# The last product of an attention and two-layer feed-forward kernel, done by Strassen's seven products on 2x2 blocks

## The chip, the cores and the metric

The kernel runs on one core of a Trainium2 chip. A core has TensorE for matrix products (PE in the profile; its weight loads are shown apart as PEld), VectorE (DVE), ScalarE (ACT), GpSimd (POOL), and SyncE (SP), which issues DMAs. Each engine runs its own queue of instructions in order, and engines wait for each other by semaphores. The metric is the time of one execution on the device, in microseconds (us); the median of three runs before the change is 658.35 us (657.65 to 659.39).

## The reference

All arrays are float32. Attention has 2 batches of 8 heads, 1152 positions and 64 dimensions per head; neighbouring queries are averaged in pairs, so 576 rows per batch come out. They are joined to x with 1152 rows and 512 columns, which goes through two feed-forward layers:

```
x  = softmax(mean_of_pairs(q) @ k.T / 8) @ v        # joined to 1152 x 512
xn = x / sqrt(mean(x*x) + 1e-6) * rms_g
y  = (silu(xn @ w_gate) * (xn @ w_val)) @ w_out      # 512 -> 1536 -> 512
h  = y @ w_in                                        # second layer: 512 -> 2048
g  = h * tanh(softplus(h))                           # mish
out = g @ w_out2                                     # 2048 -> 512
```

The change concerns the second layer: the last product, and how its two operands are prepared.

## The kernel before

To keep float32 accuracy on float16 operands, each operand is kept as two float16 halves: hi, the rounded value, and lo, what the rounding left. ScalarE writes hi (a copy), and `lo_op` (L136) writes lo as the difference of the value and hi, on GpSimd or VectorE. A product is then three matmuls: hi by hi, hi by lo, lo by hi (`mm3`, L573, and L711 to L713).

The program is written by hand in the order in which each engine gets its instructions (`tc.manual_schedule`, L785); nothing reorders it. Weights come through a line of jobs (`jobs`, `job_step`): each call of `job_step` does the last step of one job (`w_c`: hi on ScalarE, lo on GpSimd), the middle step of the next (`w_b`: two integer instructions on VectorE that put a word together from its two halves) and the first of the one after it (`w_a`: one ScalarE instruction), and starts a load ahead.

The stages, on the span's clock: attention up to about 250 us; the first layer's two products (`unit1`, 24 matmuls of 288 columns a unit) up to 395 us; the first layer's output product (`unit1o`, 16 units of 36 matmuls of 288 columns) up to 466.4 us, with the rest of the jobs for w_out and w_in beside it; and the last stage.

In the last stage the 1152 rows are taken in three chunks of 384 (`CH`). For each chunk and each of 16 blocks of 128 hidden columns (`F2`), `h_mm` (L663) does 12 matmuls of 384 columns into a PSUM bank; `h_act` (L677) applies mish on ScalarE; `h_4` (L683) writes hi on ScalarE (L686) and lo on VectorE (L687, by `lo_op`) into `g`. `o_part` (L700) multiplies 128 rows of g by two of the 16 blocks of w_out2, 512 columns a matmul, and adds up in a PSUM bank; after the last block ScalarE copies the bank out (L716) and SyncE issues the DMA to `out`. [...]

Of the kernel before, what the change touches and what calls it, by code (L numbers as in the profile page):

```python
# [35 lines left out]

# [5 lines left out]
def kernel(  # L42
# [39 lines left out]
    def pool(name, bufs, side="left", **kw):  # L82
        return tc.alloc_tile_pool(name=name, bufs=bufs, side=side, reuse_waits="tile", **kw)
# [331 lines left out]
    def w_a(job):  # L415
        t = job["raw"]
        gx = raw_p.tile([128, t.shape[1], t.shape[2]], F32, tag="gx", name="gx")
        hw = t[:, :, :, 1].bitcast(F32)
        if job.get("mish"):
            nc.scalar.activation(out=gx, in_=hw, func=ACTF.Copy, scale=2.0 ** -111)  # L420
        else:


            nc.scalar.activation(out=gx, in_=hw, func=ACTF.Prelu, scale=2.0 ** -111, alpha=-(2.0 ** 32))  # L424
        job["g"] = gx

    def w_b(job, part=None):

        t, g = job["raw"], job["g"].bitcast(I32)
        if part in (None, 0):  # L430
            job["c"] = raw_p.tile([128, t.shape[1], t.shape[2]], I32, tag="c", name="c")
        c = job["c"]
        if part in (None, 0):
            nc.vector.tensor_scalar(out=c, in0=t[:, :, :, 0], scalar1=29, scalar2=None,  # L434
                                    op0=ALU.logical_shift_right)
        if part in (None, 1):
            if job.get("mish"):
                nc.vector.scalar_tensor_tensor(out=c, in0=g, scalar=-0x80000000, in1=c,
                                               op0=ALU.bitwise_and, op1=ALU.bitwise_or)
                nc.vector.tensor_scalar(out=g, in0=g, scalar1=3, scalar2=0x7FFFFFFF,  # L440
                                        op0=ALU.logical_shift_left, op1=ALU.bitwise_and)
                nc.vector.tensor_tensor(out=c, in0=g, in1=c, op=ALU.bitwise_or)
            else:
                nc.vector.scalar_tensor_tensor(out=c, in0=g, scalar=3, in1=c,  # L444
                                               op0=ALU.logical_shift_left, op1=ALU.bitwise_or)
# [213 lines left out]
    def w2o_job(z):  # L659
        return {"load": lambda: w_load(words(w_out2)[z * 128:(z + 1) * 128, :].rearrange(  # L660
            "(k p) (f t) -> p k f t", p=128, t=2), 1),
            "to": lambda: (w2o[:, z:z + 1, 0, :], w2o[:, z:z + 1, 1, :]), "mish": True}

    gt, zt = {}, {}

    def h_mm(c, f):
        if f == 0:
            gt[c] = g_p.tile([128, F2, 2, CH], F16, tag="g", name="g")
        ps = ps_z.tile([128, 512], F32, tag="z", name="z")
        w, y1T = w2i[0], y1[0]  # L670
# [12 lines left out]
    def h_4(c, f):  # L683
        o = zt.pop((c, f))
        g = gt[c]
        nc.scalar.activation(out=g[:, f, 0, :], in_=o, func=ACTF.Copy, scale=G_S)  # L686
        lo_op(nc.vector, g[:, f, 1, :], o, G_S, g[:, f, 0, :])  # L687
# [10 lines left out]
    po_t = {}  # L698

    def o_part(c, t, part, parts):  # L700
        T = c * (CH // 128) + t
        if part == 0:
            po_t[T] = ps_o.tile([128, 512], F32, tag="o", name="po")
        ps = po_t[T]
        g = gt[c]
        n = F2 // parts
        for f in range(part * n, (part + 1) * n):
            w = w2o
            gh = g[:, f, 0, t * 128:(t + 1) * 128]
            gl = g[:, f, 1, t * 128:(t + 1) * 128]  # L710
# [3 lines left out]
        if part == parts - 1:  # L714
            o = ot_p.tile([128, DM], F32, tag="ot", name="ot")
            nc.scalar.activation(out=o, in_=ps, func=ACTF.Copy, scale=1.0 / (G_S * W_S))  # L716
            for p0, p1, dst in out_rows(T):
                nc.sync.dma_start(out=dst, in_=o[p0:p1, :])


    FL = [(0, 8), (8, 8), (16, 8), (24, 8), (32, 4)]
# [63 lines left out]
    with tc.manual_schedule():  # L785
# [113 lines left out]
        rest = [w2i_job(z) for z in range(F1 - 2 * NWB, NZ)]
        per = []  # L900
        for z in range(6, 3 * KD):
            per.append([wo_job(z)] + rest[0:1])
            rest = rest[1:]
        per += [[x] for x in rest]
# [19 lines left out]
        hs = [(c, f) for c in range(NC) for f in range(F2)]
        PARTS = 8
        NO = CH // 128
        os_ = [(c, t, p) for c in range(NC) for p in range(PARTS) for t in range(NO)]
        on = 0
        for hn in range(len(hs) + 2):
            if hn < len(hs):  # L930
                h_mm(*hs[hn])
            if 1 <= hn <= len(hs):
                h_act(*hs[hn - 1])
            if 2 <= hn:
                h_4(*hs[hn - 2])
            if jn[3] < len(jobs):
                job_step()
            goal = (hn - OLAG) * NO * PARTS // F2
            while on < min(goal, len(os_)):
                o_part(*os_[on], PARTS)  # L940
                on += 1
        while on < len(os_):
            o_part(*os_[on], PARTS)
            on += 1
        for p in (ot_p, m_p, g_p, ps_o, ps_z, w2i_p, y1_p, raw_p, const):
# [31 lines left out]
```

## Time and profile before

| | |
|---|---|
| median of three runs | 658.35 us |
| the profiled execution | 659.05 us |
| its span, first to last instruction | 657.3 us |
| PE busy | 597.6 us (91%), 5880 matmuls |
| DVE busy | 413.2 us (63%) |
| ACT busy | 391.7 us (60%) |
| POOL busy | 309.9 us (47%) |
| mean granted TensorE clock | 0.992 of full speed |

A row of the timeline gives start, duration, engine, source line, operation, written tile and read tiles, the shape, and how often it stands in a row; in square brackets stands how long the engine was idle before it and which instruction ended the wait. Matmuls overlap in the pipeline, so the time that a matmul takes from its stream is the distance of two starts, and not its duration. The execution's own time is 1.8 us longer than its span. Line numbers of the rows are those of the kernel before.

### The profile page before, as it was taken

The numbers are of one execution on the slowest core, as the hardware profiler recorded it, in microseconds if no ns is written. First come the engines' busy times: TensorE is split into PE (matmuls) and PEld (weight loads), VectorE is DVE, ScalarE is ACT, GpSimd is POOL, SyncE is SP. The second block draws the span as 40 slices with busy tenths as digits, with TensorE's granted clock in tenths as the row PEclk, the third lists the DMA queues.
The fourth block names the chain that finished last, engine by engine and source line by source line (L and its number), as shares of the span: only waits on it lengthen the run. The fifth ranks groups of instructions, "written<-read, shape, count | busy, mean of one in ns | idle before, by whom it ended". The sixth has DMA issues, their size and how long they took to land.

```text
span 657.3 us, 14631 instructions
## 1 busy us (share of the span) xinstructions
PE 597.6 (91%) x5880; PEld 419.1 (64%) x5880; DVE 413.2 (63%) x679; ACT 391.7 (60%) x661; POOL 309.9 (47%) x255
## 2 busy tenths in 40 slices
PE   3588989887887789899999999999999999999997
PEld 2366767666656567677777777777655555555553
DVE  4798989889998896568888311554499931111110
ACT  4799999998987886666666331442455533223221
POOL 0778988878896861567778420441233310000000
PEclk9899999999998999999999999999999999999999
DMA  6599999998999996545556202453244100001001
GB/s 195 133 184 202 203 192 186 210 194 183 174 209 217 181 177 143 145 145 176 172 183 192 65 1 65 130 184 105 85 140 153 41 17 32 1 2 48 1 1 48
DMA packets 161908, 84.05 MB, mean 128 GB/s; under 512 B 124720, under 2 KB 152368, under 8 KB 161840
## 3 DMA queue, kind: packets, MB, share of 16 engines
q1 hardware_dynamic: 151184, 67.71, 46.8%
q10 hardware_dynamic: 10656, 15.40, 7.8%
q8 instruction: 46, 0.75, 0.5%
q14 instruction: 22, 0.18, 0.1%
HBM read 50.07 MB, written 2.36 MB: 80 GB/s over the span
## 4 chain that ended last, share of the span: by engine, by line
PE 65%; ACT 14%; DVE 8%; issue 8%; POOL 2%; ACTq 1%; DMA 1%; DVEq 0%; POOLq 0%
ACT e L283 6%; PE z L576 5%; PE z L578 5%; PE z L577 5%; PE po L713 5%; PE po L712 5%; PE po L711 5%; PE pg L576 3%; PE pv L578 3%; PE pg L577 3%; PE pv L576 3%; PE pv L577 3%; PE pg L578 3%; PE py L576 3%; PE py L578 3%
## 5 line engine op out<-in xcount | busy, mean ns | idle before, releaser
L138 POOL TENSOR_TENSOR hl<-e,hl 128x768 f16<-128x768 f32 x71 | 117.9, 1663 | 55.8 <-ACT hl L296 26.8
L274 DVE CUSTOM_DVE_ANT_1 junk<-s,shift 128x1152 bf16<-128x1152 f32 x72 | 97.2, 1351 | 8.1 <-PE s L255 7.5
L283 ACT ACTIVATE e<-s,m 128x1152 f32<-128x1152 f32 x72 | 87.6, 1217 | 13.6 <-DVE m L274 12.8
L255 PE MATMUL s<-kqT 128*128 128x384 f16 (+1 forms) x480 | 85.4, 333 | 10.2 <-DVE kqT L209 8.1
L140 DVE SCALAR_TENSOR_TENSOR g<-mo,g 128x384 f16<-128x384 f32 x48 | 26.8, 562 | 93.3 <-ACT g L686 93.3
L138 POOL TENSOR_TENSOR stretch<-c,stretch 128x512 f16<-128x512 f32 x40 | 47.8, 1194 | 60.6 <-ACT stretch L451 60.3
L347 PE MATMUL av<-vv,et 128*128 128x65 f16 (+1 forms) x720 | 74.1, 193 | 0.9 <-DVE x L395 0.9
L349 PE MATMUL av<-vv,et 128*128 128x64 f16 (+1 forms) x720 | 74.0, 193 | 0.0
L350 PE MATMUL av<-vv,et 128*128 128x65 f16 (+1 forms) x720 | 73.9, 195 | 0.0
L347 PEld LDWEIGHTS <-et 128*128 128x128 f16 (+1 forms) x720 | 67.2, 101 | 2.4 <-issue 2.3
L349 PEld LDWEIGHTS <-et 128*128 128x128 f16 (+1 forms) x720 | 67.0, 100 | 0.7
L350 PEld LDWEIGHTS <-et 128*128 128x128 f16 (+1 forms) x720 | 67.1, 100 | 0.0
L434 DVE TENSOR_SCALAR c<-raw 128x512 int32<-128x512 int32 x68 | 48.2, 708 | 26.6 <-POOL woh L138 24.5
L138 POOL TENSOR_TENSOR h<-fo,h 128x288 f16<-128x288 f32 x48 | 45.0, 937 | 42.0 <-ACT h L613 42.0
L296 ACT ACTIVATE hl<-e 128x768 f16<-128x768 f32 x72 | 60.6, 842 | 3.9 <-POOL khl L138 1.8
L576 PE MATMUL z<-y,w2i 128*128 128x384 f16 x192 | 62.6, 326 | 0.0
L577 PE MATMUL z<-y,w2i 128*128 128x384 f16 x192 | 62.6, 326 | 0.0
L578 PE MATMUL z<-y,w2i 128*128 128x384 f16 x192 | 62.6, 326 | 0.0
L680 ACT ACTIVATE mo<-z 128x384 f32<-128x384 f32 x48 | 23.2, 484 | 64.1 <-PE z L578 63.9
L444 DVE SCALAR_TENSOR_TENSOR c<-gx,c 128x512 int32<-128x512 int32 x52 | 57.7, 1110 | 4.1 <-ACT gx L424 2.2
L255 PEld LDWEIGHTS <-kqT 128*128 128x128 f16 (+1 forms) x480 | 39.7, 101 | 31.7 <-issue 13.5
L576 PE MATMUL pg<-stretch 128*128 128x288 f16 x192 | 54.9, 286 | 2.1 <-DMA stretch<-xh 1.6
(110 smaller groups left out, 1549.1 us busy)
## 6 DMA issues: line engine op xcount, KB each, us to landing
raw<-in_moe_w_out_dram SPq DMA_DIRECT2D x28, 512.0 KB, 3.4
raw<-in_moe_w_in_dram SPq DMA_DIRECT2D x16, 512.0 KB, 3.9
raw<-in_moe_w_gate_dram SPq DMA_DIRECT2D x8, 512.0 KB, 3.5
raw<-in_moe_w_val_dram SPq DMA_DIRECT2D x8, 512.0 KB, 3.8
vn<-in_v_dram ACTq DMA_DIRECT2D x14, 288.0 KB, 4.4
kn<-in_k_dram ACTq DMA_DIRECT2D x12, 288.0 KB, 4.1
qn<-in_q_dram ACTq DMA_DIRECT2D x12, 256.0 KB, 3.8
raw<-in_moe_w_gate_dram ACTq DMA_DIRECT2D x4, 512.0 KB, 4.7
```

The source lines that it names most:

```text
L138: eng.tensor_tensor(out=out_, in0=in_, in1=hi, op=ALU.subtract)
L255: mm = nc.tensor.matmul(out=ps[p0:p0 + m, c, 0:SN], lhsT=qt[:, w * NTI + slot, p0:p0 + m], rhs=kt[:, e * NJ + c * per:e * NJ + (c + 1) * p ...
L274: nc.vector.tensor_tensor_reduce(out=junk.rearrange("p (c s) -> p c s", c=SC), in0=ps[:, :, 0:SN], in1=shift.unsqueeze(2).to_broadcast([12 ...
L283: nc.scalar.activation(out=e.rearrange("p (c s) -> p c s", c=SC), in_=ps[:, :, 0:SN], func=ACTF.Exp, bias=m, scale=s_scale)
L296: nc.scalar.activation(out=t[:, 0, :], in_=e_t[n][:, 0:NB * 128], func=ACTF.Copy)
L347: nc.tensor.matmul(out=av[0:m, o0:o0 + D + 1], lhsT=hi, rhs=vr[:, D:2 * D + 1], start=(jj == 0), stop=False)
L349: nc.tensor.matmul(out=av[0:m, o0:o0 + D], lhsT=hi, rhs=vr[:, 0:D], start=False, stop=False)
L350: nc.tensor.matmul(out=av[0:m, o0:o0 + D + 1], lhsT=et[:, z + (NB if jj < NB else PB), p0:p0 + m], rhs=vr[:, D:2 * D + 1], start=False, st ...
L444: nc.vector.scalar_tensor_tensor(out=c, in0=g, scalar=3, in1=c, op0=ALU.logical_shift_left, op1=ALU.bitwise_or)
L576: nc.tensor.matmul(out=ps, lhsT=w0, rhs=x0, start=(i == 0), stop=False)
L577: nc.tensor.matmul(out=ps, lhsT=w0, rhs=x1, start=False, stop=False)
L578: nc.tensor.matmul(out=ps, lhsT=w1, rhs=x0, start=False, stop=(i == n - 1))
```

## The change

The last product, g (1152 x 2048) by w_out2 (2048 x 512), is taken in blocks. Two blocks of 128 rows (an index `q` from 0 to 3; the ninth block of rows, `q` = 4, stays as it is) by two halves of the hidden columns, and two halves of the hidden columns by two halves of the 512 output columns, are 2x2 blocks of blocks. Plain multiplication takes eight block products for each; Strassen's scheme takes seven products of sums of blocks, and sums of the results. A block product is now 24 matmuls of 256 columns (`product`, 8 steps `i` of the halved inner length by three matmuls).

What it adds for that:
- `h_mm(q, u)` does two blocks of hidden columns for 256 rows: 24 matmuls of 256 columns into one bank; for `q` = 4, 48 matmuls of 128 columns.
- `h_act` applies mish to 512 elements, and GpSimd then makes four sums or differences of the blocks in three instructions (128, 256 and 128 elements, float32); the next two wait for the one before.
- `h_4`, three turns behind `h_mm` (before: two), writes hi and lo of seven blocks, 896 elements, instead of 384. The tile that mish and the sums share has four buffers.
- Of w_out2 three blocks are used as they are (`w2b`) and four as sums (`w2t`). `w2_sums(i)` makes the sums on VectorE (512, 256 and 256 elements, two operands in SBUF); `w2_parts(i)` writes hi on ScalarE (1024 elements) and lo on GpSimd, for i = 1, 4 and 7 on VectorE. Eight of each; the first two sums ahead of the loop, the others and the parts in its first 15 turns.
- `o_end` combines a product into the results: the first product is copied out by ScalarE (tile `p1`), the others are added by VectorE. The pool of banks for these products has three.
- The order of the seven products is such that those without sums of weights (`y` under 3) come first.
- The 16 jobs of w_out2 move into the stage before, beside `unit1o`; the remaining ten jobs of w_in move ahead of that into the first layer. [...]

The order of the loop is now: 8 turns `h` of q = 0, 8 of q = 1, 7 products of q = 0, 8 turns of q = 2, 7 products of q = 1, and so on.

```diff
-    def o_part(c, t, part, parts):
...
-            nc.tensor.matmul(out=ps, lhsT=gh, rhs=w[:, f, 0, :], start=(f == 0), stop=False)
-            nc.tensor.matmul(out=ps, lhsT=gh, rhs=w[:, f, 1, :], start=False, stop=False)
-            nc.tensor.matmul(out=ps, lhsT=gl, rhs=w[:, f, 0, :], start=False, stop=(f == F2 - 1))
...
+    def w2_sums(i):
+        b = w2f[:, i].rearrange("p h (n d) -> p (h n) d", n=2)
+        t = w2s[i] = tt_p.tile([128, 4, NHF], F32, tag="tt", name="tt")
+        for z, x, y in ((slice(0, 2), b[:, 0:1].to_broadcast([128, 2, NHF]), b[:, 1:3]), (2, b[:, 2], t[:, 0]),
+                        (3, b[:, 3], t[:, 2])):
+            nc.vector.tensor_tensor(out=t[:, z], in0=x, in1=y, op=ALU.subtract)
+    def w2_parts(i):
+        t, o = w2s.pop(i), w2t[0][:, i]
+        nc.scalar.activation(out=o[:, 0], in_=t, func=ACTF.Copy)
+        lo_op(nc.vector if i % 3 == 1 else nc.gpsimd, o[:, 1], t, 1.0, o[:, 0])
...
+            nc.scalar.activation(out=t[:, 0:4, :], in_=ps.rearrange("p (s t) -> p s t", s=4), func=ACTF.Mish, scale=sc)
+            nc.gpsimd.tensor_tensor(out=t[:, 4], in0=t[:, 0], in1=t[:, 2], op=ALU.add)
+            nc.gpsimd.tensor_tensor(out=t[:, 5:7], in0=t[:, 0:8:4], in1=t[:, 1:2].to_broadcast([128, 2, 128]), op=ALU.subtract)
+            nc.gpsimd.tensor_tensor(out=t[:, 7], in0=t[:, 3], in1=t[:, 6], op=ALU.subtract)
...
+            t = t[:, 1:8, :]
+            hi, lo = g[:, u, 0], g[:, u, 1]
+        nc.scalar.activation(out=hi, in_=t, func=ACTF.Copy, scale=G_S)
+        lo_op(nc.vector, lo, t, G_S, hi)
...
+    def product(ps, g, x, y, start, stop):
+        w, y = (w2b[0], y) if y < 3 else (w2t[0], y - 3)
+        for i in range(FP):
+            gh, gl = g[:, i, 0, x, :], g[:, i, 1, x, :]
+            wh, wl = w[:, i, 0, y, :], w[:, i, 1, y, :]
+            nc.tensor.matmul(out=ps, lhsT=gh, rhs=wh, start=start and i == 0, stop=False)
+            nc.tensor.matmul(out=ps, lhsT=gh, rhs=wl, start=False, stop=False)
+            nc.tensor.matmul(out=ps, lhsT=gl, rhs=wh, start=False, stop=stop and i == FP - 1)
+    SEVEN = [(0, 0), (2, 2), (6, 1), (5, 5), (4, 4), (3, 3), (1, 6)]
...
+        if z == 0:
+            t = keep["p1"] = ot_p.tile([128, NHF], F32, tag="p1", name="p1")
+            nc.scalar.activation(out=t, in_=ps, func=ACTF.Copy, scale=sc)
...
+        ps_z = pool("ps_z", 5, space=PSUM)
+        ps_o = pool("ps_o", 3, space=PSUM)
+        f_p = pool("f4", 4)
+        tt_p = pool("tt", 2)
...
+        for n, (kind, q, z) in enumerate(line):
+            (h_mm if kind == "h" else o_mm)(q, z)
+            if last and last[0] == "h":
+                h_act(*last[1:])
+            if len(hq) > 1 or (hq and kind == "o"):
+                h_4(*hq.pop(0))
+            if last and last[0] == "h":
+                hq.append(last[1:])
+            if last and last[0] == "o":
+                o_end(*last[1:])
+            if wp and n % 2 == 0:
+                w2_parts(wp.pop(0))
+            elif ws:
+                w2_sums(ws.pop(0))
+            last = (kind, q, z)
```

On GpSimd, at the start of the last stage, there stood only the lo halves of the weights before (stretch is where w_out2 lies):

```order
L138 TENSOR_TENSOR woh<-c,woh 128x4x128
L138 TENSOR_TENSOR w2i<-c,w2i 128x4x128 x5
L138 TENSOR_TENSOR stretch<-c,stretch 128x512 x16
L972 UNCONDITIONAL_BRANCH
L972 ISA
```

Now there stand, in the same place, the lo halves of w2b, and then, for each unit, the three sums of its tile f, with the lo halves of w2t between them:

```order
L139 TENSOR_TENSOR w2b<-stretch,w2b 128x768 x5
L139 TENSOR_TENSOR w2t<-tt,w2t 128x1024
L726 TENSOR_TENSOR f_7636<-f_7636 128x128
L727 TENSOR_TENSOR f_7636<-f_7636 128x256
L728 TENSOR_TENSOR f_7636<-f_7636 128x128
L726 TENSOR_TENSOR f_7670<-f_7670 128x128
L727 TENSOR_TENSOR f_7670<-f_7670 128x256
L728 TENSOR_TENSOR f_7670<-f_7670 128x128
```

GpSimd, which had 16 instructions in the whole stage, has its instructions of each unit between the mish and the hi half of that unit.

On VectorE a turn of the first units was, before, one lo half of g and four instructions of a w_out2 job:

```order
L140 SCALAR_TENSOR_TENSOR g<-mo,g 128x384
L434 TENSOR_SCALAR c<-raw 128x512
L438 SCALAR_TENSOR_TENSOR c<-gx,c 128x512
L440 TENSOR_SCALAR gx<-gx 128x512
L442 TENSOR_TENSOR c<-gx,c 128x512
```

Now it is the lo half of g, larger, and in every second turn the sums of weights in tile tt; here are the turns that follow the lo half of part 1:

```order
L139 TENSOR_TENSOR w2t<-tt,w2t 128x1024
L141 SCALAR_TENSOR_TENSOR g<-f_7636,g 128x896
L679 TENSOR_TENSOR tt<-stretch 128x512
L679 TENSOR_TENSOR tt<-stretch,tt 128x256 x2
L141 SCALAR_TENSOR_TENSOR g<-f_7670,g 128x896
L141 SCALAR_TENSOR_TENSOR g<-f_7702,g 128x896
L679 TENSOR_TENSOR tt<-stretch 128x512
L679 TENSOR_TENSOR tt<-stretch,tt 128x256 x2
```

Every one of these instructions reads two operands from SBUF.

On ScalarE, around the first products, these rows stand now (f4 is the tile of mish and sums, stretch the g of q = 1, p1 the copy of the first product); the first two hi halves are those of the units 13 and 14, the third that of unit 15:

```order
L740 ACTIVATE stretch_89<-f4_8085 128x896
L740 ACTIVATE stretch_89<-f4_8119 128x896
L802 ACTIVATE p1_8186<-po_8126 128x256
L740 ACTIVATE stretch_89<-f4_8151 128x896
L725 ACTIVATE f4_8379<-z_8327 128x512
L725 ACTIVATE f4_8409<-z_8354 128x512
```

Before, a copy of a finished bank stood there every 16 units and more (L716); now the copy of the first product's bank stands behind the hi half of unit 14.

## Rows read from the trace of the kernel before

**Rows 1.** Busy time by stretch: stretch, length, PE, PEld, DVE, ACT, POOL, clock, DMA.
```profile
500.00:520.00 20.00, 20.00 (x109) 10.52 (x108) 19.41 (x28) 10.82 (x23) 6.55 (x6) 1.00 0.30 106
580.00:600.00 20.00, 20.00 (x109) 10.53 (x108) 2.58 (x5) 3.61 (x8) 0.00 (x0) 1.00 0.00 1
```
**Rows 2.** Groups of PE in the last stage: count, busy us, mean ns, idle.
```profile
L576 PE MATMUL z<-y,w2i 128*128 128x384 f16 x192 | 62.6, 326 | 0.0
...
L711 PE MATMUL po<-stretch,g 128*128 128x512 f16 x144 | 54.6, 379 | 0.0
```
**Rows 3.** Timeline of PE: start, duration, at several places of the span.
```profile
201.10 0.28 PE L204 MATMUL s<-ident,khl 128*128 128x128 f16 x2
...
201.55 0.28 PE L318 MATMUL ep<-idf,e 128*128 128x128 f32 x1
...
466.39 0.33 PE L576 MATMUL z<-y,w2i 128*128 128x384 f16 x1
...
644.81 0.38 PE L711 MATMUL po<-stretch,g 128*128 128x512 f16 x1
...
653.01 0.38 PE L713 MATMUL po<-stretch,g 128*128 128x512 f16 x1
```
**Rows 4.** Timeline of DVE and POOL where both work on SBUF.
```profile
414.94 1.16 POOL L138 TENSOR_TENSOR w2i<-c,w2i 128x512 f16<-128x512 f32 x1
417.92 1.71 POOL L138 TENSOR_TENSOR woh<-c,woh 128x512 f16<-128x512 f32 x1 [1.82 <-ACT woh L451]
...
415.02 1.36 DVE L434 TENSOR_SCALAR c<-raw 128x512 int32<-128x512 int32 x1 [16.02 <-POOL woh L138]
...
417.46 0.42 DVE L434 TENSOR_SCALAR c<-raw 128x512 int32<-128x512 int32 x1
417.91 0.69 DVE L444 SCALAR_TENSOR_TENSOR c<-gx,c 128x512 int32<-128x512 int32 x1
...
19.11 1.64 POOL L138 TENSOR_TENSOR hl<-e,hl 128x768 f16<-128x768 f32 x1 [17.17 <-ACT hl L296]
20.70 1.62 POOL L169 TENSOR_TENSOR qs<-qn 128x576 f32<-128x576 f32 x1
...
19.91 1.16 DVE L145 TENSOR_SCALAR kn<-kn 128x576 f32<-128x576 f32 x1
```
**Rows 5.** Durations: groups of ACT and DVE, and one line of POOL (ns, min/median/max).
```profile
L686 ACT ACTIVATE g<-mo 128x384 f16<-128x384 f32 x48 | 24.7, 516 | 0.0
...
L296 ACT ACTIVATE hl<-e 128x768 f16<-128x768 f32 x72 | 60.6, 842 | 3.9 <-POOL khl L138 1.8 <-ACT e L283 0.2
...
L140 DVE SCALAR_TENSOR_TENSOR g<-mo,g 128x384 f16<-128x384 f32 x48 | 26.8, 562 | 93.3 <-ACT g L686 93.3
...
L442 DVE TENSOR_TENSOR c<-gx,c 128x512 int32<-128x512 int32 x16 | 11.1, 693 | 0.6
...
L169 POOL TENSOR_TENSOR qs<-qn x7: 1397/1414/1845, 20.7 to 190.8; 128x576 f32<-128x576 f32 x7
```
**Rows 6.** Timeline at the start of the last stage.
```profile
466.59 0.41 ACT L644 ACTIVATE y<-py 128x288 f16<-128x288 f32 x1 [4.00 <-PE py L578]
...
467.02 1.28 ACT L923 ACT_TABLE_LOAD   x1
...
467.86 0.69 DVE L444 SCALAR_TENSOR_TENSOR c<-gx,c 128x512 int32<-128x512 int32 x1
```
**Rows 7.** Timeline of PE in the first layer's output product.
```profile
434.84 0.29 PE L578 MATMUL py<-h,woh 128*128 128x288 f16 x1
435.29 0.28 PE L576 MATMUL py<-h,woh 128*128 128x288 f16 x1 [0.16 <-DVE y L140]
```
**Rows 8.** Busy time by stretch, as in rows 1, where the clock changes.
```profile
26.60:33.20 6.60, 5.23 (x22) 2.81 (x21) 3.88 (x8) 4.89 (x8) 5.71 (x4) 0.50 0.67 151
202.70:206.10 3.40, 0.81 (x10) 0.39 (x7) 3.40 (x5) 0.92 (x2) 1.12 (x2) 1.00 1.17 244
207.50:210.70 3.20, 3.20 (x34) 2.16 (x31) 2.20 (x4) 3.17 (x5) 1.91 (x2) 0.50 0.92 237
```

More of the change, by code (lines that the diff above doesn't have):

```diff
@@ L32 @@
 NE, JOB0, JOBL = 4, 59, 55
-OLAG = 6
 PB = 3
@@ L418, in w_a @@
         hw = t[:, :, :, 1].bitcast(F32)
[L419 to L424, printed above, removed]
+        nc.scalar.activation(out=gx, in_=hw, func=ACTF.Prelu, scale=2.0 ** -111, alpha=-(2.0 ** 32))
         job["g"] = gx
@@ L436, in w_b @@
         if part in (None, 1):
[L437 to L445, printed above, removed]
+            nc.vector.scalar_tensor_tensor(out=c, in0=g, scalar=3, in1=c,
+                                           op0=ALU.logical_shift_left, op1=ALU.bitwise_or)
             del job["raw"], job["g"]
     def w_c(job):
+        if "to" not in job:
+            job["end"]()
+            return
         hi, lo = job["to"]()
@@ L669, in h_mm, with col0, g_buf @@
+    gt, zt = {}, {}
+    NQ = NT // 256
+    def col0(q):
+        return NI * 128 if q == NQ else q * 256 + (128 if q >= NI // 2 else 0)
+    def g_buf(q):
+        if q not in gt:
+            if q % 2:
+                gt[q] = stretch[:, 0:FP * 2 * 7 * 128].rearrange("p (i w s t) -> p i w s t", i=FP, w=2, s=7)
+            else:
+                gt[q] = g_p.tile([128, FP, 2, 7, 128], F16, tag="g", name="g")
+        return gt[q]
+    def h_mm(q, u):
         ps = ps_z.tile([128, 512], F32, tag="z", name="z")
@@ L683, in h_4 @@
[L683 to L687, printed above, removed]
+        n = 128 if q == NQ else 256
+        cs = slice(col0(q), col0(q) + n)
+        fs = [u + FP * h for h in range(2)] if n == 256 else [i + FP * h for i in (2 * u, 2 * u + 1) for h in range(2)]
+        for z, f in enumerate(fs):
+            mm3(ps[:, z * n:(z + 1) * n], lambda i: (w[:, i, 0, f * 128:(f + 1) * 128], w[:, i, 1, f * 128:(f + 1) * 128]),
+                lambda i: (y1T[:, i, 0, cs], y1T[:, i, 1, cs]), KD)
@@ L689, in out_rows, with h_4 @@
+    def h_4(q, u):
+        t = zt.pop((q, u))
+        g = g_buf(q)
+        if q == NQ:
+            t = t[:, 0:6, :].rearrange("p (i s) t -> p i s t", i=2)
+            hi, lo = [g[:, 2 * u:2 * u + 2, w, 0:3, :] for w in range(2)]
+        else:
+            t = t[:, 1:8, :]
+            hi, lo = g[:, u, 0], g[:, u, 1]
+        nc.scalar.activation(out=hi, in_=t, func=ACTF.Copy, scale=G_S)
+        lo_op(nc.vector, lo, t, G_S, hi)
     def out_rows(T):
@@ L696, in out_rows @@
         return [(0, TL, out[TB - TL:TB, :]), (TL, 128, out[2 * TB - TL:2 * TB, :])]
-    po_t = {}
-    def o_part(c, t, part, parts):
[L701 to L710, printed above, removed]
-            nc.tensor.matmul(out=ps, lhsT=gh, rhs=w[:, f, 0, :], start=(f == 0), stop=False)
-            nc.tensor.matmul(out=ps, lhsT=gh, rhs=w[:, f, 1, :], start=False, stop=False)
-            nc.tensor.matmul(out=ps, lhsT=gl, rhs=w[:, f, 0, :], start=False, stop=(f == F2 - 1))
-        if part == parts - 1:
-            o = ot_p.tile([128, DM], F32, tag="ot", name="ot")
-            nc.scalar.activation(out=o, in_=ps, func=ACTF.Copy, scale=1.0 / (G_S * W_S))
+    acc, keep = {}, {}
@@ new lines, with o_mm, o_end, plus @@
+    SEVEN = [(0, 0), (2, 2), (6, 1), (5, 5), (4, 4), (3, 3), (1, 6)]
+    ODD = [(0, 0), (1, 2), (2, 1), (0, 4)]
+    def o_mm(q, z):
+        x, y = (ODD if q == NQ else SEVEN)[z]
+        if q < NQ or z % 2 == 0:
+            acc[q] = ps_o.tile([128, 512], F32, tag="o", name="po")
+        product(acc[q][:, 0:NHF], gt[q], x, y, q < NQ or z % 2 == 0, q < NQ or z % 2 == 1)
+        acc[q, z] = acc[q][:, 0:NHF]
+    def o_end(q, z):
+        ps = acc.pop((q, z))
+        sc = 1.0 / (G_S * W_S)
+        def plus(to, x):
+            if isinstance(to, str):
+                t = keep[to] = ot_p.tile([128, NHF], F32, tag=to, name=to)
+            else:
+                t = to
+            nc.vector.scalar_tensor_tensor(out=t, in0=ps, scalar=sc, in1=keep[x], op0=ALU.mult, op1=ALU.add)
+        def send(T, o):
@@ L890 @@
             jobs += [wo_job(f - 2 * NWB), w2i_job(f - 2 * NWB), w1_job(f, 0), w1_job(f, 1)]
+        jobs += [w2i_job(z) for z in range(F1 - 2 * NWB, NZ)]
         units = [(f, c) for f in range(NWB) for c in range(NH // B + 1, NH)]
@@ L898 @@
         unit1_end(*done1[-1])
[L899 to L904, printed above, removed]
+        jw = [w2o_job(i, h) for i in range(FP) for h in range(2)]
+        jo = [wo_job(z) for z in range(6, 3 * KD)]
+        turns = "ww w o ow o ww o ow o ww ww w w w w w".split()
+        for x in "".join(turns):
+            jobs.append((jo if x == "o" else jw).pop(0))
         outs = [(d, c) for d in range(KD) for c in range(NH)]
@@ L907 @@
             unit1o(d, c)
-            if i < len(per):
-                jobs += per[i]
-                job_step(len(per[i]))
+            job_step(len(turns[i]))
             if i:
@@ L913 @@
         unit1o_end(*outs[-1])
-        jobs += [w2o_job(z) for z in range(F2)]
-        for p in (ps_f, ps_t, ps_av, wo_p, h1_p, h0_p, ftm):
+        job_step(2)
+        for p in (ps_f, ps_t, ps_av, wo_p, h1_p, h0_p, ftm, raw_p):
             p.release()
@@ L918 @@
         ps_o = pool("ps_o", 3, space=PSUM)
-        g_p = pool("g", 2)
-        m_p = pool("m", 3)
-        ot_p = pool("ot", 2)
-        nc.scalar.preload_act_table_set("mish")
[L924 to L945, printed above, removed]
+        w2t_p = pool("w2t", 1)
+        w2t[0] = w2t_p.tile([128, FP, 2, 4, NHF], F16, tag="w2t", name="w2t")
+        g_p = pool("g", 1)
+        f_p = pool("f4", 4)
+        tt_p = pool("tt", 2)
+        ot_p = pool("ot", 1)
+        nc.scalar.preload_act_table_set("mish")
+        line = []
+        for q in range(NQ + 1):
+            line += [("h", q, u) for u in range(FP if q < NQ else FP // 2)]
+            if q:
+                line += [("o", q - 1, z) for z in range(7)]
+        line += [("o", NQ, z) for z in range(4)]
+        hq, last = [], None
+        for i in range(2):
+            w2_sums(i)
+        wp, ws = list(range(FP)), list(range(2, FP))
+        for n, (kind, q, z) in enumerate(line):
[13 more added lines that the diff above has]
+            last = (kind, q, z)
+        o_end(*last[1:])
+        for p in (ot_p, tt_p, f_p, g_p, w2t_p, ps_o, ps_z, w2b_p, w2i_p, y1_p, const):
             p.release()
```

79 lines of the change are left out of this document (60 added, 19 removed).

## The prediction

> **What bounds the kernel now.** I read the table by stretch first: in the last stage PE is busy for 20.00 us of each 20, at full clock, both while the weights' jobs still keep DVE at 19.41 and after them, when DVE needs 2.58 and POOL nothing [rows 1]. So the stage lasts as long as PE's stream, and the other engines have room. Then the groups of PE: 3 x 192 matmuls of 384 columns and 3 x 144 of 512 [rows 2]. Then the distances of starts in the timeline: 38 matmuls of 512 columns from 644.81 to 653.01, 216 ns each; eight of 128 columns from 201.10 to 201.55, 56 ns each [rows 3]. Both are columns/2.4 plus about 2.5 ns, so 384 columns take 162.5 ns and 256 take 109.2. Check: 576 x 0.1625 + 432 x 0.2159 = 186.9 us; from 466.39, the stage's first matmul, that gives 653.3, where the last one of 653.01 ends its turn [rows 3]. Last I looked where DVE and POOL work side by side.
>
> **PE's own work.** After: h takes 768 matmuls of 256 and 192 of 128 columns, 768 x 0.1092 + 192 x 0.056 = 94.6 us; the products take 28 x 24 + 4 x 24 = 768 of 256, 83.9. Together 178.5, so PE saves 8.4 us if it never waits.
>
> What goes out of the stage, the w_out jobs with DVE's 19.41 of 20 us, was hidden under PE's full stream [rows 1] and brings nothing by itself.
>
> **The stage before.** PE lost 0.33 us at 434.84 to 435.29, where a bank was late: its reader came after a wait of ScalarE for a weight buffer [rows 7]. The jobs of w_out now stand in later turns, behind more of those readers; I count 0.3 saved. The other moved jobs run beside PE's full stream; nothing of them is waited for before their last, at the stage's start.
>
> **What DVE and POOL do to each other.** A POOL instruction of 512 elements takes 1.16 us; the one at 417.92, started 0.01 after a DVE one of 0.69 with two SBUF operands, took 1.71: it ended 1.02 after DVE's end. A DVE instruction of 0.42, started at 415.02 beside POOL's of 414.94, took 1.36 and ended 0.28 after POOL's. So one waits for the whole of the other, and hides only 0.14 us of its own in the wait. Where POOL has a queue, they take turns: DVE's of 19.91 ended 0.32 after POOL's first, and POOL's second took 1.62 where 1.40 is the least [rows 4, 5]. The change's new instructions on both engines are of this kind.
>
> Durations. POOL: 512 and 768 elements take 1.16 and 1.64 [rows 4], 1.9 ns an element and 0.18 us; with two float32 operands 576 take 1.40 [rows 5], 2.12 ns an element. So 128, 256 and 128 take 0.45 + 0.72 + 0.45 = 1.62 a unit, and a lo half of 1024 2.14. That no row shows float32 sums this small is a bound: at 1.9 ns a unit takes 1.51. DVE: 384 take 0.562 and 512 take 0.693 [rows 5], 1.04 ns an element and 0.16, so SBUF is held 0.93 for 896 and 1.07 for 1024. ScalarE: 384 in 0.516, 768 in 0.842 [rows 5], so 896 in 0.95, 1024 in 1.06. With some 0.6 for a mish of 512 ScalarE needs 0.95 + 0.6 and every second turn 1.06, some 2.1 of PE's 2.62 a turn: it is late only where it waits.
>
> **Where it is late.** Time 0 is the first matmul of the stage; a turn of PE is 24 x 0.1092 = 2.62 us. The first products need g of q = 0, ready with unit 7, half way through the sum below. The latest thing is a bank: the fourth product takes the bank of the first, which ScalarE reads into p1, in its queue behind the hi half of unit 14, and that waits for POOL's sums of unit 14. PE is there after 16 units and three products, at 19 x 2.62 = 49.8.
>
> POOL's start: y's hi half begins at 0.2, the last job's word is ready on DVE at 2.2 (467.86 + 0.69) [rows 6]; ScalarE's w2b half 0.84, POOL's lo of it 1.64, to 4.8. Beside it ScalarE loads its table, 1.28, to 4.4; DVE makes the first weight sums, held up by that POOL instruction, to about 5.2; w2t's hi half 1.06; POOL begins with w2t at 6.4. To the end of unit 14 it has five lo halves and 15 units: 5 x 2.14 + 15 x 1.62 = 35.0. In that time DVE takes SBUF for 14 lo halves of g, six sums of weights and three lo halves of w2t: 14 x 0.93 + 6 x 1.07 + 3 x 1.07 = 22.7, in 14 + 18 + 3 = 35 instructions, and each wait hides 0.14: 4.9. So POOL ends unit 14 at 6.4 + 35.0 + 22.7 - 4.9 = 59.2. With 0.08 to start, hi of 0.95, and p1's 256 elements in 0.37, the bank is free at 60.6: PE waits 10.8 us.
>
> Bounds of that. If POOL's start-up parts always fell into DVE's turns, and its sums went at 1.9 ns, POOL needs 45 x 0.04 + 15 x 0.97 + 5 x 2.0 + 22.7 = 49.1, and PE waits 7.1. If none is hidden, 57.7 + 6.4 = 64.1, and it waits 15.7. A gain from the wait is excluded, since p1 cannot pass in ScalarE's queue. I take 10.8, nearest to the rows, where waits did hide 0.14. After it POOL needs less than a turn (1.62 + 0.93 against 2.62, and the seven products give it 18 us more), so I expect no second wait of this size.
>
> **The clock.** PE was idle for most of 202.7 to 206.1, at a granted clock of 1.00; in 207.5 to 210.7, with PE full again, it was 0.50, the lower of the two levels, 1.2 GHz; an earlier stretch at that level, 26.6 to 33.2, is twice as long [rows 8]. After a wait of ten us I expect the same, 3.2 to 6.6 us of work at half rate, 1.6 to 3.3 us lost. I take 2.5.
>
> **The end.** The last copy is 0.2 shorter; a second DMA (the ninth block of rows goes to two places) is issued behind it. Bounds -0.4 and +0.4; I take 0.
>
> **Sum.** -8.4 - 0.3 + 10.8 + 2.5 = +4.6 us. Against the profiled execution, 659.05, that is 663.6 (its span 657.3 to 661.9). The median of the runs is 0.7 lower: 662.9.
>
> **Rivals.**
> A second forecast, faster: POOL and DVE take no turns, or POOL's float32 sums slip between. Place: the same bank. POOL's queue alone ends at 6.4 + 35.0 = 41.4, p1 at 42.8, ahead of PE's 49.8. It decides from the point where POOL ends unit 14 before 48.4. Then only -8.7 is left: 649.7. For it: with DVE at 19.41 and POOL at 6.55 of 20 us PE still ran full [rows 1]. Against it: each pair in rows 4. The Trainium skill (GPSIMD Engine Reference, Specifications) has the two share SBUF interfaces just for DVE instructions with two SBUF operands or in a two-port mode; it gives no price, and the pairs above agree with it.
> Part of it: a third of the holds costs POOL nothing, so they add 11.9 instead of 17.8. POOL ends unit 14 at 53.3, the bank is free at 54.7, PE waits 4.9, and the clock costs 1.6: -8.7 + 6.5 = -2.2, 656.2. For it: POOL also rests while DVE waits for ScalarE, so not all holds meet a waiting POOL. Against: POOL's queue in this time has no rest, by the sum.
> The change doesn't do what it says, since weight loads set the pace of short matmuls. A load is busy for 10.52/108 = 97 ns [rows 1]; under 109 that hides, but the 192 matmuls of 128 columns would take 97 instead of 56: 7.9 us on top of the forecast, 670.8. Against: eight such matmuls, each with its load, at 56 ns [rows 3].
> The Trainium skill (TensorE: Matmul & The Clock Gate, Back-to-back issue gap) speaks for this rival: it gives a stream of load and matmul 81 ns at 128 columns, by which these 192 would cost 4.8 us more, and 131 at 512; the trace has 56 and 216, so it does not bear the rule out.
> Worse: nothing hides, 15.7, and the clock costs 3.3: -8.7 + 19.0 = 10.3, 668.7.
>
> **How the numbers follow.** Forecast (PE waits 7.1 to 13.4) 0.60; no wait 0.14; a part of it 0.15; worse 0.09; slow matmuls 0.02. What a measurement of this kernel can tell from no change is about 0.3%, 2 us: faster is under 656.4, slower over 660.3. No wait and half of the part case, which lies on the line, make 0.22 faster; its other half and 0.12 of the forecast, at its low end (-8.7 + 7.1 + 1.6 = 0.0, 658.4), make 0.19 same; 0.59 are slower. The forecast's own range is 658.4 to 666.4 (-8.7 + 13.4 + 3.3); to leave no more than 2 in 10 out, the range goes down past the part case to 655.8 and up to the worse, 668.8.
>
> **What would show it.** In the profile after: one idle stretch of PE, near 49.8 us into the last stage, at the fourth product, ended by ScalarE's p1; POOL busy without rest from 6 to 60 us into the stage, its instructions of 128 elements well above 0.45 us on the mean and DVE's lo of 896 above 1.09; a granted clock of 0.5 behind the stretch; starts of 256-column matmuls 109 ns apart everywhere else; no wait of that kind at the later products. If POOL's instructions show 0.45 and 0.72, the forecast's ground is wrong; if PE waits for w2t's lo halves and not for the bank, only its place.

## The result and the profile after

The changed kernel takes 664.1 us (median of 6 runs, 662.4 to 665.8) against 658.4 us of the kernel before on the same chip: ratio 1.008 (95% interval 1.0054 to 1.0105), 0.8% slower. The forecast was 662.9 us. The profiled execution took 665.06 us, its span is 663.2 us.

The first view to read is again busy time by stretch, now of the last stage (length, PE, PEld, DVE, ACT, POOL, clock, DMA; the rows that answer to [rows 1]):

```profile
466.30:516.00 49.70, 49.70 (x457) 44.52 (x456) 37.58 (x40) 27.34 (x36) 43.08 (x42) 1.00 0.01 1
516.00:527.40 11.40, 0.27 (x3) 0.10 (x1) 5.96 (x5) 5.67 (x8) 10.80 (x12) 0.64 0.00 0
527.40:532.90 5.50, 5.46 (x26) 3.78 (x26) 2.80 (x5) 0.95 (x1) 1.18 (x1) 0.50 0.00 0
532.90:540.00 7.10, 7.10 (x68) 6.36 (x65) 1.79 (x5) 0.00 (x0) 0.00 (x0) 1.00 0.08 31
540.00:600.00 60.00, 60.00 (x552) 53.79 (x550) 20.20 (x22) 20.34 (x29) 31.03 (x44) 1.00 0.04 15
600.00:658.60 58.60, 58.60 (x633) 53.60 (x631) 15.13 (x24) 9.69 (x15) 6.77 (x9) 1.00 0.05 19
```

PE is full in every stretch but one: from 516.0 to 527.4, some 11 us, it does nothing, and the 5.5 us behind run at a clock of 0.50. The only engine without rest in the idle stretch is POOL: 10.80 of 11.40. In the 49.70 us ahead it is busy for 43.08, with most of the rest before its first w2t half. The list of PE's waits in the stage has one row (line, what ended it, us, times, longest):

```profile
PE po L760 <- ACT p L802: 11.2, 1, 11.2
```

ScalarE's timeline around the end of the wait (start, duration, what; the kernel before had no such copy) shows what p1's copy stands behind:

```profile
523.69 0.95 ACT L740 ACTIVATE stretch<-f 128x896 f16<-128x896 f32 x1 [1.04 <-POOL f L728]
526.17 0.95 ACT L740 ACTIVATE stretch<-f 128x896 f16<-128x896 f32 x1 [1.52 <-POOL f L728]
527.02 0.37 ACT L802 ACTIVATE p<-po 128x256 f32<-128x256 f32 x1
```

ScalarE waits for POOL's last sum (L728), then does hi of unit 14 and, right behind it, the copy that frees the bank. So the bank is late because POOL's queue is. POOL's groups in the first part of the stage, 466.3 to 530 (to be held against the 0.45, 0.72 and 0.45 us that the prediction worked out from [rows 4, 5]):

```profile
L727 POOL TENSOR_TENSOR f<-f 128x256 f32<-128x256 f32 x16 | 18.7, 1168 | 1.3
L728 POOL TENSOR_TENSOR f<-f 128x128 f32<-128x128 f32 x16 | 13.6, 850 | 1.3
L726 POOL TENSOR_TENSOR f<-f 128x128 f32<-128x128 f32 x16 | 11.1, 694 | 0.0
L139 POOL TENSOR_TENSOR w2t<-tt,w2t 128x1024 f16<-128x1024 f32 x5 | 10.8, 2151 | 1.5 <-ACT w2t L683 1.5
```

The lines of the three sums from 540 on, where VectorE has no weights left to sum:

```profile
L728 POOL TENSOR_TENSOR f<-f 128x128 f32<-128x128 f32 x16 | 16.0, 1003 | 1.3
L727 POOL TENSOR_TENSOR f<-f 128x256 f32<-128x256 f32 x16 | 11.6, 725 | 1.2
L726 POOL TENSOR_TENSOR f<-f 128x128 f32<-128x128 f32 x16 | 7.3, 454 | 38.2 <-ACT f L725 37.2
```

There the first two sums take what was worked out, and only the third meets VectorE's lo half of the unit before: it takes 1.18 us in 12 of the 16 units and 0.46 in the other four. In the first part all three are held up: a unit takes 2.7 us, where 1.62 is what it needs. VectorE pays too: its lo halves of 896 elements take 1.39 us in that part, where 1.09 was worked out:

```profile
L141 DVE SCALAR_TENSOR_TENSOR g<-f,g 128x896 f16<-128x896 f32 x8 | 11.0, 1390 | 0.1
```

How the two meet is seen in two pairs of the timelines, POOL's first:

```profile
522.48 1.18 POOL L728 TENSOR_TENSOR f<-f 128x128 f32<-128x128 f32 x1
...
524.95 1.18 POOL L728 TENSOR_TENSOR f<-f 128x128 f32<-128x128 f32 x1
```

```profile
522.20 1.15 DVE L141 SCALAR_TENSOR_TENSOR stretch<-f,stretch 128x896 f16<-128x896 f32 x1 [2.12 <-ACT stretch L740]
524.68 1.15 DVE L141 SCALAR_TENSOR_TENSOR stretch<-f,stretch 128x896 f16<-128x896 f32 x1 [1.33 <-ACT stretch L740]
```

The POOL instruction of 524.95 began 0.27 us after VectorE's, and ended at 526.13, 0.30 behind VectorE's end at 525.83: of its 0.45 us only 0.15 passed during the wait, as in [rows 4]. The pair before it shows the same: begun 0.28 after VectorE's, ended 0.31 behind its end.

PE's own pace and the end of the program, from two places of the timeline (rows that answer to [rows 3]):

```profile
619.82 0.22 PE L573 MATMUL z<-y,w2i 128*128 128x128 f16 x1
...
621.43 0.22 PE L575 MATMUL z<-y,w2i 128*128 128x128 f16 x1
...
657.70 0.27 PE L760 MATMUL po<-w2t,g 128*128 128x256 f16 x1
...
658.58 0.27 PE L762 MATMUL po<-w2t,g 128*128 128x256 f16 x1
658.88 0.38 ACT L795 ACTIVATE ot<-po 128x256 f32<-128x256 f32 x1 [4.86 <-PE po L762]
659.29 1.19 SPq L788 DMA_DIRECT2D out_dram<-ot  x2
```

From 619.82 to 621.43 stand 29 steps of 56 ns at 128 columns, from 657.70 to 658.58 eight of 110 ns at 256, each matmul with a weight load of its own. That is the pace of their columns that the prediction took.

### The profile page after: what moved, and what is told of

It reads as the page before. It is cut to its first block, busy times and chain, and to the rows that moved or that the text cites. A ratio compares the mean times of both kernels' runs of the same rounds, so it can differ in the third digit from the quotient of the medians.

```text
span 663.2 us, 16171 instructions
## 1 busy us (share of the span) xinstructions
PE 590.9 (89%) x6600; PEld 481.8 (73%) x6600; DVE 453.0 (68%) x694; ACT 403.2 (61%) x634; POOL 398.0 (60%) x352
## 4 chain that ended last, share of the span: by engine, by line
PE 57%; ACT 14%; POOL 9%; issue 9%; DVE 8%; DMA 2%; ACTq 1%; DVEq 0%; POOLq 0%
ACT e L284 6%; PE po L760 4%; PE po L761 4%; PE po L762 4%; PE py L575 4%; PE py L574 4%; PE py L573 4%; PE pg L573 3%; PE pv L575 3%; PE pv L574 3%; PE pv L573 3%; PE pg L575 3%; PE pg L574 3%; DVE junk L275 3%; POOL f L727 3%
## 5 line engine op out<-in xcount | busy, mean ns | idle before, releaser
L574 PE MATMUL z<-y,w2i 128*128 128x256 f16 (+1 forms) x320 | 80.6, 262 | 0.0
L575 PE MATMUL z<-y,w2i 128*128 128x256 f16 (+1 forms) x320 | 80.6, 262 | 0.0
L573 PE MATMUL z<-y,w2i 128*128 128x256 f16 (+1 forms) x320 | 80.5, 262 | 0.0
L438 DVE SCALAR_TENSOR_TENSOR c<-gx,c 128x512 int32<-128x512 int32 x52 | 64.1, 1233 | 3.2 <-ACT gx L422 1.4
L139 POOL TENSOR_TENSOR h<-fo,h 128x288 f16<-128x288 f32 x48 | 48.1, 1001 | 21.2 <-ACT h L610 21.2
L573 PE MATMUL pv<-stretch 128*128 128x288 f16 x192 | 54.9, 286 | 0.0
L574 PE MATMUL pv<-stretch 128*128 128x288 f16 x192 | 54.9, 286 | 0.0
L575 PE MATMUL pv<-stretch 128*128 128x288 f16 x192 | 54.9, 286 | 0.0
L573 PE MATMUL py<-h,woh 128*128 128x288 f16 x192 | 54.9, 286 | 0.0
```

## The experiments

The theory is this: POOL's instructions and VectorE's with two operands in SBUF exclude each other, so POOL's queue of sums and w2t halves is done only 60 us into the stage, and the first product's bank, read behind it, is late. The rivals: GpSimd is too slow by itself; the banks and the place of p1's copy make the wait whatever the other engines do. The runs of the kernel before that stood beside the eight kernels were at 659.06 us for the first four and at 660.04 for the last four; so the ratios are what to compare. An expected time over 658.4 us gives the expected ratio.

**VectorE's low half from PSUM.** One of the two operands in SBUF is taken from VectorE's lo halves of g, and nothing is taken from GpSimd. The kernel leaves out the true lo halves of mish and of its sums, so it counts for its time alone.

```diff
-        lo_op(nc.vector, lo, t, G_S, hi)
+        if q == NQ:
+            lo_op(nc.vector, lo, t, G_S, hi)
+        else:
+            z, sc = ps.rearrange("p (s t) -> p s t", s=4), 1.0 / (Y_S * W_S)
+            lo_op(nc.vector, lo[:, 0:4, :], z, G_S * sc, hi[:, 0:4, :])
+            lo_op(nc.vector, lo[:, 4:7, :], z[:, 0:3, :], G_S * sc, hi[:, 4:7, :])
```

> The changed kernel with one thing altered: VectorE's low half of g (896 elements, both operands in SBUF) is made by two instructions of 512 and 384 elements whose first operand is the PSUM bank of z, so that it holds what z holds and not the low half of mish and its sums. GpSimd's instructions are the same in kind, number and size. Theory (GpSimd's sums and VectorE's instructions with two SBUF operands exclude each other): GpSimd's three sums of a unit fall from 0.69/1.17/0.85 us to near the means they have with VectorE quiet (0.45/0.73/0.45), the wait of 11.3 us at the fourth product shrinks below 1 us, the clock stays up, and the time is 664.1 - 11.3 - 2.7 = 650.1 us (649 to 652). Rival 1 (GpSimd is too slow by itself): its means stay, the wait stays within 1.5 us of 11.3, time 662 to 665. Rival 2 (the place of p1's copy in ScalarE's queue and the count of banks alone): the wait stays too, 662 to 665.

Measured: 653.8 us, ratio 0.9929 (0.9908 to 0.9951). GpSimd's groups in the first part of the stage:

```profile
L727 POOL TENSOR_TENSOR f<-f 128x256 f32<-128x256 f32 x16 | 14.8, 924 | 1.3
L139 POOL TENSOR_TENSOR w2t<-tt,w2t 128x1024 f16<-128x1024 f32 x5 | 10.8, 2157 | 1.5 <-ACT w2t L683 1.5
L728 POOL TENSOR_TENSOR f<-f 128x128 f32<-128x128 f32 x16 | 8.8, 549 | 1.3
L726 POOL TENSOR_TENSOR f<-f 128x128 f32<-128x128 f32 x16 | 8.6, 538 | 0.0
```

The same 16 units of the same sums take 32.2 us in place of 43.4, and the wait at the fourth product is gone, against both rivals. In this part VectorE's sums and lo halves of weights still read SBUF twice. From 540 on, where they are done and VectorE has only its lo halves, the three sums are at what was worked out:

```profile
L727 POOL TENSOR_TENSOR f<-f 128x256 f32<-128x256 f32 x13 | 9.4, 725 | 1.0
L728 POOL TENSOR_TENSOR f<-f 128x128 f32<-128x128 f32 x14 | 6.4, 455 | 1.1
L726 POOL TENSOR_TENSOR f<-f 128x128 f32<-128x128 f32 x13 | 5.9, 457 | 29.1 <-ACT f L725 29.1
```

The third sum, 1.00 us on the mean in the changed kernel, is at 0.455, though it still runs beside VectorE's lo halves. So the lo half that reads one operand from PSUM holds GpSimd up no longer, and that settles what the first part leaves open.

The time, 653.8 us, lies above the expected 649 to 652; by the ratios, 0.9929 for 0.9874, 3.6 us are missing. The list of PE's waits says what I had left out:

```profile
PE z L573 <- DVE g L141: 2.5, 4, 1.2
PE z L573 <- DVE stretch L141: 0.2, 1, 0.2
```

A low half that reads z keeps z's bank some us longer than mish does, and five times a unit had to wait for a bank, 2.7 us in all. The rest, 0.9 us, is within the interval.

**The three parts of the queue, one at a time.** Sums of g to VectorE; w2t's halves to VectorE; the ends of a product ahead of the unit's own work.

```diff
-            nc.gpsimd.tensor_tensor(out=t[:, 4], in0=t[:, 0], in1=t[:, 2], op=ALU.add)
+            nc.vector.tensor_tensor(out=t[:, 4], in0=t[:, 0], in1=t[:, 2], op=ALU.add)
...
```

(so also the other sums of `h_act`)

> The changed kernel with g's sums (three instructions of a unit) by VectorE in place of GpSimd; GpSimd keeps only the low halves of w2t (two of three). Theory (exclusion): what was GpSimd's queue is now VectorE's, shorter by the faster sums but still shared with GpSimd's w2t halves: a wait of 6 to 8 us at the fourth product in place of 11.3, time 664.1 - 3.8 = 660.3 us (657.5 to 661.5, the low end if the clock falls later or not at all). Rival (GpSimd is too slow by itself, VectorE has room): no wait, 650 us. Rival (VectorE's queue is now the longer): the wait is over 11 us, 664 us or more.

```diff
-        lo_op(nc.vector if i % 3 == 1 else nc.gpsimd, o[:, 1], t, 1.0, o[:, 0])
+        lo_op(nc.vector, o[:, 1], t, 1.0, o[:, 0])
```

> The changed kernel with all eight low halves of w2t by VectorE (three of eight before); g's sums stay on GpSimd. Theory (exclusion): five GpSimd instructions of 2.15 us go out of its queue, five of 1.56 us or less enter VectorE's, and the two still wait for each other: the wait at the fourth product is 5 to 6 us plus about 1 at the fifth, time 664.1 - 5.7 = 658.4 us with the clock's loss, 655.7 without it (655 to 659). Rival (GpSimd too slow by itself): its queue of 16 units by 1.7 us is done before PE asks, no wait, 650 us. Rival (the order of p1's copy and the banks alone): the wait stays at 11 us, 664 us.

```diff
+            if last and last[0] == "o":
+                o_end(*last[1:])
             if last and last[0] == "h":
                 h_act(*last[1:])
...
-            if last and last[0] == "o":
-                o_end(*last[1:])
```

> The changed kernel with one thing moved: in each slot what follows a product (p1's copy on ScalarE, the sums with p1 on VectorE) is written ahead of the unit's mish and high half, so that p1's copy stands one high half earlier in ScalarE's queue. Theory (GpSimd's queue is late, p1's copy waits behind what GpSimd releases): the wait falls by one unit's turn, 2.5 us, from 11.3 to 8 to 9 us, time 664.1 - 2.5 = 661.6 us (660.5 to 662.5). Rival (the order of p1's copy and the banks alone make the wait): it goes, 650 us. If neither, the wait moves on to the next products in full and the time stays at 664.

| run | time, us | ratio (interval) | expected ratio | wait at the fourth product, us |
|---|---|---|---|---|
| sums by VectorE | 659.7 | 1.0014 (1.0000 to 1.0027) | 1.003 | 7.0 |
| w2t by VectorE | 658.6 | 0.9993 (0.9982 to 1.0004) | 1.000 | 5.7 |
| product's end first | 661.9 | 1.0045 (1.0030 to 1.0059) | 1.005 | 8.7 |

Each has one wait, where the changed kernel has it. The rows, one list for each of the three kernels in the order of the table:

```profile
PE po L760 <- ACT p L802: 7.0, 1, 7.0
```

```profile
PE po L760 <- ACT p L802: 5.7, 1, 5.7
```

```profile
PE po L760 <- ACT p L802: 8.7, 1, 8.7
```

Every wait lies in the range that the theory's queue gave, and no rival's 650 or 664 us came. The second short wait that I had counted, about 1 us at the fifth product, did not come. With the sums on VectorE, POOL has five w2t halves and nothing else, and the wait is still 7.0 us: there VectorE's queue is the long one, so it is the two engines' common work that is too much for the first 50 us, and not GpSimd's alone. The w2t run says it the other way round. GpSimd's sums take longer still, 48.0 us in all for 43.4, since VectorE now has more that excludes them (466 to 530):

```profile
L727 POOL TENSOR_TENSOR f<-f 128x256 f32<-128x256 f32 x16 | 18.2, 1135 | 1.3
L726 POOL TENSOR_TENSOR f<-f 128x128 f32<-128x128 f32 x16 | 15.6, 975 | 2.1 <-ACT f L725 2.1
L728 POOL TENSOR_TENSOR f<-f 128x128 f32<-128x128 f32 x16 | 14.2, 889 | 1.3
```

and the queue is done earlier all the same: a lo half of 1024 elements takes GpSimd 2.15 us, and VectorE 1.22 where nothing holds it up (the three of the run with the sums on VectorE).

**The banks.**

```diff
-        ps_z = pool("ps_z", 5, space=PSUM)
-        ps_o = pool("ps_o", 3, space=PSUM)
+        ps_z = pool("ps_z", 4, space=PSUM)
+        ps_o = pool("ps_o", 4, space=PSUM)
```

> The changed kernel with four banks for z and four for the products (five and three before). Theory (the wait is for GpSimd's late queue, the bank only says which product meets it): the wait moves on to the fifth product and is shorter by about one product (2.6 us) and a little: 7 us there, 1 us at the sixth, a short one of under 1 us at a z, time 664.1 - 2.7 = 661.4 us (659.5 to 662.5). Rival (too few banks for the products are the cause): no wait, 650 us. Rival (z's banks were the scarce ones): new waits at z of over 3 us in all, 664 us or more.

Measured: 661.8 us, ratio 1.0030 (1.0016 to 1.0045; expected 1.005). PE's waits in the stage:

```profile
PE po L760 <- ACT p L802: 6.9, 1, 6.9
PE z L573 <- ACT f L725: 0.9, 1, 0.9
PE po L761 <- DVE w2t L139: 0.2, 1, 0.2
```

The 6.9 us stand one product later (PE stops 53.9 us into the stage in place of 49.7), and 0.9 us at a z bank came in. The 1 us that I had expected at the sixth product did not come. The bank only says which product meets the late queue.

One other count of buffers was not tried. In the first part of the stage VectorE waits 10.1 us for GpSimd to free a tile of weight sums, of which there are two (`tt_p`):

```profile
L679 DVE TENSOR_TENSOR tt<-stretch 128x512 f32<-128x512 f32 x8 | 7.0, 871 | 10.1 <-POOL w2t L139 10.1
```

GpSimd's own queue has hardly a rest there all the same, so by the theory more tiles would not shorten it; no run shows it.

**A version without the wait.** Two ways to it, and a control that has the order of the second but not w2t by VectorE.

> Three edits together, the order of the products unchanged: w2t's low halves all by VectorE, four banks for the products and four for z, and what follows a product written ahead of the unit's mish and high half. Theory (the three shorten one wait by 5.5, 2.6 and 2.5 us of its 11.3): about 1 us of wait is left, at the fifth or sixth product, the clock stays up, 650.1 + 1 = 651.1 us (650 to 653). Rival (a second limit takes over, so that the parts do not add): a wait of 5 us or more is left, 657 to 659 us.

The new order of products, in the loop that writes `line`; with it each block's first four products stand one behind each of the last four z units of the next:

```diff
-            line += [("h", q, u) for u in range(FP if q < NQ else FP // 2)]
-            if q:
-                line += [("o", q - 1, z) for z in range(7)]
+            H = [("h", q, u) for u in range(FP if q < NQ else FP // 2)]
+            O = [("o", q - 1, z) for z in range(7 if q else 0)]
+            while H or O:
+                if H:
+                    line.append(H.pop(0))
+                if O and len(H) <= 3:
+                    line.append(O.pop(0))
```

> w2t's low halves all by VectorE, what follows a product written ahead of the unit's mish and high half, and the products of one block laid between the last four z units of the next (after the fifth unit one product, one unit, and so on; banks five and three as in the changed kernel). Theory (GpSimd's queue is too long only where a block's products come in one piece behind sixteen units; spread, each unit's sums are done before PE asks): no wait over 0.5 us after the first unit, 650.1 us (649.3 to 651.5). Rival (the first product, asked for 10 us earlier, meets g's sums of the first block late): a wait of 2 to 4 us at the first product, 652 to 655 us. Rival (GpSimd and VectorE together are over PE's pace in every block): the wait comes back in later blocks, 655 us or more.

> As the run with the spread products and the earlier product ends, but w2t's low halves stay as in the changed kernel (five of eight on GpSimd). Theory (the order of the products mends part, GpSimd's load the rest): 3 us of wait inside the first product and about 1.3 us at the fifth, 650.1 + 4.4 = 654.5 us (652.5 to 656). Rival (the order alone was at fault): no wait, 650 us. Rival (GpSimd's load alone): a wait of over 8 us somewhere in the first block, 661 us or more.

| run | time, us | ratio (interval) | expected ratio | PE's waits, us |
|---|---|---|---|---|
| 4 + 4 banks, end first, w2t by VectorE | 652.2 | 0.9883 (0.9867 to 0.9898) | 0.989 | 0.6 and 0.9 |
| spread order, end first, w2t by VectorE | 650.9 | 0.9859 (0.9845 to 0.9873) | 0.987 | none |
| spread order, end first | 656.1 | 0.9936 (0.9924 to 0.9949) | 0.994 | 3.1 and 1.5 |

The last one's waits, as its trace lists them:

```profile
PE po L762 <- DVE g L141: 3.1, 1, 3.1
PE po L760 <- DVE ot L784: 1.5, 1, 1.5
```

The order alone doesn't do it: the first product, asked for earlier, meets the last lo half of g, which is late by the same queue. With w2t off GpSimd as well PE has no wait in the stage; its stretches:

```profile
466.30:516.00 49.70, 49.70 (x457) 44.53 (x456) 47.07 (x48) 30.11 (x40) 42.35 (x41) 1.00 0.01 1
516.00:540.00 24.00, 24.00 (x222) 21.50 (x221) 9.89 (x14) 7.71 (x12) 14.22 (x21) 1.00 0.06 23
540.00:600.00 60.00, 60.00 (x552) 53.77 (x551) 22.61 (x27) 19.79 (x28) 27.37 (x37) 1.00 0.03 10
600.00:644.70 44.70, 44.70 (x506) 41.11 (x503) 8.72 (x17) 6.19 (x10) 2.90 (x4) 1.00 0.07 25
```

PE's 178.40 us here are the 178.5 that the prediction counted for PE's own work in the stage, 186.8 in the kernel before. This version beats both kernels: by the ratios 1.4% under the one before, where the changed kernel is 0.8% over it.

## Why the prediction was right

Its own steps, in its order; measured from the two profiled executions (659.05 and 665.06 us).

- **PE's own work**, -8.4 us: right. The version without waits has the 178.4 us, the spacing is 56 and 110 ns, and the rival of slow short matmuls is out by the rows of 128 columns. By them the rule of the Trainium skill (TensorE: Matmul & The Clock Gate, Back-to-back issue gap), 81 ns at 128 columns, does not hold here.
- **The stage before**, -0.3: PE's work from its first output matmul to the last stage took 70.6 us for 71.1. The bank of [rows 7] is no longer late, and a second late one, at 439.58, that the prediction had not counted (0.23 us) is gone too: some -0.55. The work began 0.5 later, so the stage starts at 466.33 for 466.39 [rows 3]; -0.1 in all. That later beginning can't be put down to the change: in the eight further runs, whose programs are the same up to there, it lies anywhere from 394.1 to 396.9, while the 70.6 us stand in each.
- **POOL's queue**, PE 10.8 us idle at 49.8 us into the stage: measured 11.2 at 49.7, at the fourth product, ended by p1's copy. The exclusion behind it is shown by the PSUM run, the length of the queue by the three runs that shorten it, the place by the run with four banks. The Trainium skill (GPSIMD Engine Reference, Specifications) has the two engines share their way to SBUF for such instructions, and the runs agree; that section gives no price, and the sum's came from rows. It stood on little: of the three pairs in [rows 4] only the first has a VectorE instruction with two operands in SBUF, the kind that the change brings. The sum took each hold of VectorE in full, less 0.14 a wait. From its first w2t half, 6.35 us into the stage (6.4 in the sum), to the end of unit 14's sums, at 59.8 (59.2), POOL took 53.5 us, with just the five halves, 15 units and VectorE's 35 instructions that were counted. Against the 35.0 without holds that is 18.5 more, where 17.8 were worked out. Some of that nearness is luck: the instructions themselves grew by 16.8 us, and the other 1.7 are pauses between them, some 0.08 us ahead of each second and third sum of a unit, which the sum had left out. The case of a part of it (PE waits 4.9 us) took a third of the holds as free; they were not, since POOL's queue had hardly a rest.
- **The clock**, 2.5 us: 5.5 us at 0.50, half of it lost, 2.7.
- **The end**, 0 within 0.4: the last matmul's turn ends at 658.7, the span at 663.2, 4.5 us for 4.0 before. That is 0.5, just over its bound: the step that was off. The rows of the end in the kernel before, to be held against the last two of the timeline above:

```profile
653.61 0.60 ACT L716 ACTIVATE ot<-po 128x512 f32<-128x512 f32 x1 [0.88 <-DMA out_dram<-ot]
654.23 0.33 SPq L718 DMA_DIRECT2D out_dram<-ot  x1
```

  The copy now ends 0.4 us sooner behind the last matmul's turn. But the one DMA of before was issued 0.35 us after the copy's end, and of the two now the second 1.2 us after it. From there to the end of the span it is 2.7 us in both. So the second DMA costs 0.9, more than the 0.4 that the shorter copy gives back.

Sum: -8.4 - 0.1 + 11.2 + 2.7 + 0.5 = +5.9 us; the spans differ by 5.9, the medians by 5.7, and +4.6 was forecast. The miss of 1.3 us is 0.4 of wait, 0.2 of clock, 0.2 of the stage before (by its chance beginning) and 0.5 at the end.

What the forecast had said of the later products, no second wait of this size, holds: VectorE's weights are done by then, and the list of waits has one row.

## What to carry to other kernels

A change that takes work from the engine that bounds a stage and gives it to two engines that share something must be counted as one queue: add up what each holds of the shared thing until the moment at which the bound engine asks, and compare that with the time it takes to get there. Work of weights that is needed once falls on the first block alone, so look at the start of the stage and not at its mean; there the remedies are the cheaper of the two engines for the shared work, and consumers spread between producers, so that no bank is asked for before its reader's turn. Moving an instruction to the other engine of the two gains only what its hold gets shorter by it: the sums moved to VectorE left 7.0 of 11.2 us of wait, w2t's halves 5.7. Taking one operand from PSUM took VectorE's lo halves out of the common queue altogether; whether a kernel that keeps the accuracy can do so, no run shows.

## What was not expected of the hardware

The clock's loss did not follow the length of the wait, in one profiled execution of each kernel. Behind 5.7 us without work (w2t by VectorE) the granted clock was 0.50 for 3.8 us of work (stretches as in the first fence, of that run):

```profile
516.00:521.80 5.80, 0.32 (x3) 0.14 (x2) 2.34 (x3) 2.25 (x4) 5.41 (x8) 0.74 0.00 0
521.80:525.60 3.80, 3.58 (x17) 2.45 (x17) 2.47 (x4) 1.12 (x2) 1.32 (x2) 0.50 0.00 0
525.60:530.00 4.40, 4.40 (x42) 3.94 (x41) 1.54 (x5) 0.00 (x0) 0.00 (x0) 1.00 0.00 0
```

Behind 8.7 us it was 0.50 for 4.7 us, behind 7.0 and 11.2 for 5.5. The run with the spread order alone, which waited 3.1 us and later 1.5, stayed at full clock:

```profile
503.90:523.00 19.10, 16.02 (x147) 14.11 (x146) 13.41 (x12) 9.44 (x13) 18.24 (x19) 1.00 0.00 1
523.00:540.00 17.00, 15.47 (x143) 13.68 (x141) 7.29 (x12) 5.33 (x8) 9.03 (x13) 1.00 0.09 32
```

I had allowed for no loss at all behind the waits of 5.7 and 7.0 us; it was 1.9 and 2.7, half of the stretches.
